# Attention in rounds of four chunks, with one scaling per output group and GpSimd copying the gate's columns

## The chip, the core and the metric

The kernel runs on one core of a Trainium2 chip. The metric is device time in microseconds for one launch. One execution was also recorded by the hardware profiler; all durations below come from that recording.

## The reference

The computation is a linear attention over 8 batches, 8 heads, 576 positions and head dimension 64, followed by a mixture of 8 experts with sticky routing:

```python
def phi(x):                                   # 64 -> 128 -> 256 features
    proj = x @ w_phi
    proj = proj - max(abs(proj), axis=-1)
    return concatenate([exp(proj), exp(-proj)])
kv  = einsum('bhsf,bhsd->bhfd', phi(k), v)
z   = sum(phi(k), axis=s)
out = (phi(q) @ kv) / (phi(q) @ z + 1e-6)     # (B, H, S, D) -> x (B, S, 512)
# per token: logits = x @ w_gate; a local gate decides between argmax(logits)
# and the expert of the token before; p = softmax; out = p[e] * (relu(x @ w1[e]) @ w2[e])
```

All inputs and outputs are float32.

## The kernel before

**Attention.** Two batches and two heads form a unit; there are 16 units (`NBP` x `NHP`), each of 9 chunks (`NC`) of 128 positions, 144 chunks in all. Chunk 4 of a unit is split between the two batches, called b = 0 and b = 1. Two consecutive chunks form a pair, 72 pairs. The order of TensorE's instructions is written out by hand; the other engines are ordered by a scheduler that respects the data and the buffers.

`step(p)` is called once per pair and issues on TensorE, in this order:

- `proj(p)`: the projections of keys and queries of a pair into the tile `pj` (2 PSUM buffers). VectorE takes the maximum of absolute values (`m`, L186) and subtracts it (`sb`, L188); ScalarE makes the key features `kp` (L192).
- `qtr(p-1)`: four transposes of the queries' part into `qt` (1 PSUM buffer), from which ScalarE makes the query features `qp` (two instructions, L206; 8 buffers).
- `turn` and then `gate` of what became ready in earlier steps: when the last chunk of a unit's batch half has been summed, `kv_end` copies the sum out (ScalarE, `kf` and `kvs`). `turn`, one step later, transposes it (L251) into a PSUM tile `nm` and ScalarE copies that out (`ks`, L254). `gate`, again one step later, multiplies it with the gate's weights (L263) into another `nm` tile, and ScalarE copies the nine columns into `kvs` (L265). This tile then also receives the first group of outputs.
- `kv` of the two chunks of pair p-2 (L225, tile `kvp`).
- up to `QUOTA` = 18 entries of the list `todo`. An entry is one matrix multiplication of `num` (two records in the profile, L284), eight entries per chunk. A `num` covers two or three chunks and one `nm` tile; there are four per unit, on chunks (0,1), (2,3), (4,5,6) and (7,8). Its last entry, `end`, issues the scaling: VectorE adds 1e-6 to the denominators (L301), inverts them (L302), scales the 64 output columns of both heads into `xo` (L306) and the nine gate columns into `lg` (L308); one DMA on SyncE's queue writes `xo` to the tensor `xs` (L312).
- what `kv` has left after a unit's half was completed, and then the background work: the routing of a finished pair of batches (`gate(bp)`, a generator started by `ends`, which is an entry of `todo` too), and early preparation of experts. It advances piece by piece, has small matrix multiplications into a tile that shares the one PSUM buffer of `qt` (`pst`), and loads and splits expert weights (L753, L754).

The `nm` tiles have **two** PSUM buffers, shared by `turn`, `gate` and `num`. GpSimd scatters the routing lists and gathers tokens with indirect DMAs; `paced` puts a small copy (`tick`, L387) in front of each of these, which waits for `m`.

**Experts.** After the attention come the expert slots: each loads 4 MB of weights, splits them in a high and a low part on ScalarE and VectorE (L753, L754), and TensorE multiplies in three products (L799 to L801).

Of the kernel before, what the change touches and what calls it, by code (L numbers as in the profile page):

```python
# [6 lines left out]
F32 = mybir.dt.float32  # L7
# [9 lines left out]
B, H, S, D = 8, 8, 576, 64  # L17
# [10 lines left out]
WAIT = 5  # L28
LAG = 2
WE, WR, WL = 8, 4, 1  # L30
FILL = 6
KVLAG = 2
QUOTA = 18

STEP = "step"

# [10 lines left out]
class Kernel:  # L47
# [9 lines left out]
    def run(self):  # L57
        nc, tc, A = self.nc, self.tc, self.A
        act, dve = self.act, self.dve
        with ExitStack() as root:  # L60
            self.const = self.mkpool(root, "const", 1, "left")
            dram = self.mkpool(root, "dram", 1, "left", DRAM)
            self.xs = dram.tile([NT + 1, DM], F32, name="xs")

            self.lst = dram.tile([E * NT + 128, 2], F32, name="lst")
            first = self.const.tile([128, 256], F32, name="first")
            self.sp.dma_start(first[:, 128:256], A["first"][:, 384:512])
            self.ident, self.w2 = first[:, 0:128], first[:, 128:256]
            self.cnt = self.const.tile([128, E], BF16, name="cnt")
            dve.memset(self.cnt, 0.0)  # L70

            warm = self.const.tile([128, E], BF16, name="warm")
            act.activation(warm, self.cnt, AF.Exp)

            self.wgi = self.const.tile([128, NHP, 2, 9], F32, name="wgi")
            self.pool.memset(self.wgi, 0.0)

            self.vs = [[self.const.tile([128, 2, D + 1], F32, name=f"vs{k}{b}") for b in (0, 1)] for k in (0, 1)]
            for x in self.vs:
                for t in x:  # L80
# [12 lines left out]
            self.psf = self.mkpool(front, "psf", 2, "right", PSUM)  # L93
            self.wphases = [(self.moe_early, WE)]

            self.scattering = False
            self.tail, self.eslots, self.scattered = False, [], []
            self.g, self.ch, self.kvb, self.lg = {}, {}, {}, {}
            n = NBP * NHP * NC
            self.todo, self.turns, self.gates, self.background = [], [], [], []  # L100
            self.fetched = 0
            for gi in range(3):
                self.fetch_kqv(gi)
                if gi == 0:
                    self.sp.dma_start(first[:, 0:128], A["first"][:, 256:384])
                    self.consts()
            with tc.manual_schedule(engines={mybir.EngineType.PE}):
                for p in range(n // 2):
                    while self.fetched < n // 3 and self.fetched * 3 < 2 * p + 8:
                        self.fetch_kqv(self.fetched)  # L110
                    if p == FILL:
# [3 lines left out]
                    self.step(p, n)  # L115
            self.tail = True
            p = n // 2
            while p < n // 2 + KVLAG + 1 or self.todo or self.turns or self.gates:
                self.step(p, n)
                p += 1  # L120
# [51 lines left out]
    def proj(self, p):  # L172

        dve, act = self.dve, self.act

        t = self.psf.tile([128, 2, 2, 2, 128], F32, name="pj")
        for i in (2 * p, 2 * p + 1):
            kq = self.g[i // 3]["kq"]
            s = slice(i % 3 * 128, i % 3 * 128 + 128)
            for j in (0, 1):  # L180
                for h in (0, 1):
                    r = slice(64 * h, 64 * h + 64)
                    self.last_pe = self.pe.matmul(t[:, h, i % 2, j, :], kq[r, j, s], self.w2[r], start=True, stop=True)  # L183
        m = self.m = self.front3.tile([128, 8], F32, name="m")
        f = t.rearrange("p h c j f -> p (h c j) f")
        dve.tensor_reduce(m, f, AX.X, ALU.max, apply_absolute_value=True)  # L186
        sb = self.front3.tile([128, 2, 2, 2, 128], F32, name="sb")
        self.last_dve = dve.tensor_sub(sb.rearrange("p h c j f -> p (h c j) f"), f,  # L188
                                       m.unsqueeze(2).broadcast_to([128, 8, 128]))
        kp = self.front3.tile([128, 2, 2, 2, 128], F32, name="kp", bufs=4)  # L190
        for sg in (0, 1):
            self.last_act = act.activation(kp[:, :, :, sg, :].rearrange("p c h f -> p h c f"), sb[:, :, :, 0], AF.Exp,  # L192
                                           scale=1.0 - 2 * sg)
        for c in (0, 1):
            self.ch[2 * p + c] = dict(kp=kp[:, c], sb=sb)
# [76 lines left out]
    def num(self, u, b, cs, kvs, bank=None):  # L272
# [22 lines left out]
        def end():  # L295
            last()
            dve, t = self.dve, e["t"]
            for c in cs:
                del self.ch[u * NC + c]
            rc = self.back2.tile([128, 3, 2], F32, name="rc", bufs=3)[:, 0:n]  # L300
            dve.tensor_scalar_add(rc, t[:, :, :, D], 1e-6)  # L301
            dve.reciprocal(rc, rc)  # L302
            if hp == 0 and c0 == 0:
                self.lg[bp] = self.back2.tile([128, NC, 9, H], F32, name="lg")
            xo = self.back2.tile([128, 3, 128], F32, name="xo", bufs=4)[:, 0:n]
            dve.tensor_mul(xo.rearrange("p c (h d) -> p c h d", h=2), t[:, :, :, 0:D],  # L306
                           rc.unsqueeze(3).broadcast_to([128, n, 2, D]))
            dve.tensor_mul(self.lg[bp][:, c0:c0 + n, :, 2 * hp:2 * hp + 2].rearrange("p c e h -> p c h e"),  # L308
                           t[:, :, :, D + 1:KV], rc.unsqueeze(3).broadcast_to([128, n, 2, 9]))
            r0 = bp * TB + c0 * 128  # L310
            dst = self.xs[r0:r0 + n * 128, hp * 128:hp * 128 + 128].rearrange("(c p) d -> p c d", p=128)
            self.sp.dma_start(dst, xo)  # L312
        self.todo.append(end)

    def ends(self, bp):
# [29 lines left out]
                self.load(s, i)  # L345
            yield

    def step(self, p, n):

        if p < n // 2:  # L350
            self.proj(p)
        if 0 <= p - 1 < n // 2:
            self.qtr(p - 1)
        gates, self.gates = self.gates, []
        turns, self.turns = self.turns, []
        for x in turns:
# [1 line left out]
        for x in gates:  # L358
            x()
        parts = [[]]  # L360
        if 0 <= p - KVLAG < n // 2:
            for i in (2 * (p - KVLAG), 2 * (p - KVLAG) + 1):
                a, *more = self.kv(i)
                parts[-1] += a
                parts += more
        for x in parts[0]:
            x()
        for _ in range(min(QUOTA, len(self.todo)) if p < n // 2 else len(self.todo)):
            self.todo.pop(0)()
        for part in parts[1:]:  # L370
            for x in part:
                x()
        for x in list(self.background):
            for _ in range(6):
                y = next(x, self)
                if y is self:
                    self.background.remove(x)
                if y is self or y is STEP:
                    break

    def paced(self):
# [5 lines left out]
        return self.tc.issue_after(self.pool.tensor_copy(t, self.m[:, 0:1]).ins)  # L387


    def pst(self, shape):  # L390
# [617 lines left out]
```

## Time and profile before

| | |
|---|---|
| median of 3 runs | 834.18 us (828.74 to 838.76) |
| profiled execution, its own time | 827.13 us |
| its span, first to last instruction | 825.4 us |
| TensorE matmuls busy | 788.1 us (95%) |
| VectorE busy | 555.4 us (67%) |
| ScalarE busy | 428.2 us (52%) |
| GpSimd busy | 146.7 us (18%) |
| attention | about the first 335 us of the span |

Busy time is the union of an engine's instructions; matmuls are pipelined, so a TensorE that is busy all the time may still be waiting for short spells. The weight loads of TensorE (PEld) are shown beside its matmuls (PE) and show its issue rhythm more sharply. "Released by" names the work whose end let an instruction start; "issue" is idle time for which the profile shows no cause.

### The profile page before, as it was taken

Reading aid. Unit: us, or ns where it says so; the run is one execution under the profiler, and the core shown is the slowest. Engines: PE = TensorE matmul, PEld = TensorE weight load, DVE = VectorE, ACT = ScalarE, POOL = GpSimd, SP = SyncE. Lnnn points to the kernel's source line nnn. Section 1 sums busy time; section 2 is a strip of 40 time slices with the busy share of each in tenths; the row PEclk is TensorE's granted clock in tenths of the full one; section 3 lists DMA queues with packets and bytes.
Section 4 is the critical chain, followed back from the end, with each engine's and each line's share of the span. In section 5 each row is a group of like instructions: output and inputs, shape, how many; then the busy total and the mean of one; then the engine's idle time right before and its main releaser. Section 6 shows DMA issues by size and latency. Waiting matters only on the chain.

```text
span 825.4 us, 23470 instructions
## 1 busy us (share of the span) xinstructions
PE 788.1 (95%) x9777; PEld 710.0 (86%) x9777; DVE 555.4 (67%) x956; ACT 428.2 (52%) x738; POOL 146.7 (18%) x156
## 2 busy tenths in 40 slices
PE   6999998999989899888999999999999999999997
PEld 5899987898878788777898998998898898999896
DVE  5677897679878885848754444644686777568541
ACT  4666665566666565323543333533564557447431
POOL 0000002200231132051421202212122212201010
PEclk9999999999999999999999999999999999999999
DMA  6545546764799531574974433744696687767510
GB/s 193 141 123 135 144 130 92 124 149 126 151 215 236 168 102 36 157 138 136 393 255 141 162 116 121 286 141 148 207 346 211 209 319 263 257 224 273 192 44 23
DMA packets 74239, 145.01 MB, mean 176 GB/s; under 512 B 9198, under 2 KB 48757, under 8 KB 74112
## 3 DMA queue, kind: packets, MB, share of 16 engines
q1 hardware_dynamic: 66272, 123.14, 50.9%
q0 software_dynamic: 7792, 20.02, 7.2%
q8 instruction: 79, 1.29, 0.7%
q10 hardware_dynamic: 64, 0.30, 0.1%
q14 instruction: 32, 0.26, 0.1%
HBM read 124.51 MB, written 20.26 MB: 175 GB/s over the span
## 4 chain that ended last, share of the span: by engine, by line
PE 69%; issue 12%; DMA 7%; DVE 6%; ACT 2%; POOL 2%; another core or an unknown queue 1%; SPq 1%; POOLq 0%; DVEq 0%; ACTq 0%
PE l L799 12%; PE l L800 12%; PE l L801 12%; PE kvp L225 8%; PE pj L183 8%; PE nm L284 8%; PE qt L203 4%; DMA out<-y,p_tokm 4%; DMA wraw<-in_w2h 2%; PE tr L791 1%; DVE sb L188 1%; DVE m L186 1%; PE nm L263 1%; POOL out L874 1%; DMA p_lrm<-lst,p_rim 1%
## 5 line engine op out<-in xcount | busy, mean ns | idle before, releaser
L753 ACT CAST whi<-wraw 128x1024 fp32r<-128x1024 f32 x160 | 167.5, 1048 | 205.7 <-PE l L801 111.6
L754 DVE TENSOR_TENSOR wlo<-wraw,whi 128x1024 fp32r<-128x1024 f32 x160 | 195.7, 1224 | 85.9 <-ACT whi L753 83.6
L799 PE MATMUL l<-xhi,whi 128*128 128x256 f32 x544 | 155.2, 286 | 2.1 <-DVE hl L822 1.4
L800 PE MATMUL l<-xlo,whi 128*128 128x256 f32 x544 | 152.8, 281 | 0.3 <-DVE xlo L794 0.3
L801 PE MATMUL l<-xhi,wlo 128*128 128x256 f32 x544 | 152.4, 280 | 0.0
L799 PE MATMUL l<-whi,hh 128*128 128x512 f32 x320 | 127.4, 398 | 0.7 <-DVE y L873 0.7
L800 PE MATMUL l<-wlo,hh 128*128 128x512 f32 x320 | 125.8, 393 | 0.0
L801 PE MATMUL l<-whi,hl 128*128 128x512 f32 x320 | 125.7, 393 | 0.0
L186 DVE TENSOR_REDUCE m<-pj 128x8 f32<-128x1024 f32 x72 | 87.9, 1220 | 43.9 <-PE pj L183 43.7
L206 ACT ACTIVATE qp<-qt 128x512 f32<-128x512 f32 x144 | 84.7, 604 | 60.3 <-PE qt L203 57.9
L192 ACT ACTIVATE kp<-sb 128x512 f32<-128x512 f32 x144 | 82.9, 623 | 54.2 <-DVE sb L188 46.5
L799 PEld LDWEIGHTS l<-xhi,whi 128*128 128x128 f32 x544 | 102.8, 189 | 4.5 <-DVE hl L822 1.9
L800 PEld LDWEIGHTS l<-xlo,whi 128*128 128x128 f32 x544 | 102.8, 189 | 1.1 <-DVE xlo L794 0.5
L801 PEld LDWEIGHTS l<-xhi,wlo 128*128 128x128 f32 x544 | 102.9, 189 | 0.0
L284 PE MATMUL nm<-kvs,qp 128*64 128x74 f32 x2304 | 89.0, 230 | 6.8 <-ACT kvs L265 4.8
L183 PE MATMUL pj<-first,kq 64*128 64x128 f32 x1152 | 86.9, 291 | 8.1 <-DMA kq<-in_kqT 6.4
L874 POOL DMA_INDIRECT out<-y,p_tokm x34 | 44.4, 1305 | 269.2 <-DVE y L873 250.7
L188 DVE TENSOR_TENSOR sb<-pj,m 128x1024 f32<-128x1024 f32 x72 | 88.1, 1224 | 3.7
L284 PEld LDWEIGHTS nm<-kvs,qp 128*64 128x64 f32 x2304 | 81.2, 139 | 8.1 <-ACT kvs L265 5.3
L183 PEld LDWEIGHTS pj<-first,kq 64*128 64x128 f32 x1152 | 72.6, 193 | 13.9 <-issue 6.8
L225 PE MATMUL kvp<-v,kp 128*64 128x65 f32 x2048 | 78.1, 227 | 0.5 <-ACT kvs L245 0.4
L225 PEld LDWEIGHTS kvp<-v,kp 128*64 128x64 f32 x2048 | 68.5, 140 | 6.6 <-issue 5.4
(200 smaller groups left out, 1000.3 us busy)
## 6 DMA issues: line engine op xcount, KB each, us to landing
wraw<-in_w1h SPq DMA_DIRECT2D x80, 512.0 KB, 5.9
wraw<-in_w2h SPq DMA_DIRECT2D x80, 512.0 KB, 4.4
kq<-in_kqT SPq DMA_DIRECT2D x47, 384.0 KB, 4.6
v<-in_va SPq DMA_DIRECT2D x48, 195.0 KB, 3.0
xs<-xo SPq DMA_DIRECT2D x48, 128.0 KB, 4.1
xs<-xo SPq DMA_DIRECT2D x16, 192.0 KB, 2.1
vs<-in_va SPq DMA_DIRECT2D x32, 32.5 KB, 3.0
lst<-pr,ri POOLq DMA_INDIRECT x36, 6.3
```

Source lines behind the costliest of these rows:

```text
L183: self.last_pe = self.pe.matmul(t[:, h, i % 2, j, :], kq[r, j, s], self.w2[r], start=True, stop=True)
L186: dve.tensor_reduce(m, f, AX.X, ALU.max, apply_absolute_value=True)
L188: self.last_dve = dve.tensor_sub(sb.rearrange("p h c j f -> p (h c j) f"), f, m.unsqueeze(2).broadcast_to([128, 8, 128]))
L192: self.last_act = act.activation(kp[:, :, :, sg, :].rearrange("p c h f -> p h c f"), sb[:, :, :, 0], AF.Exp, scale=1.0 - 2 * sg)
L206: self.act.activation(qp[:, sg], t, AF.Exp, scale=1.0 - 2 * sg)
L225: self.pe.matmul(self.kvp[r, sg, h], self.ch[i]["kp"][:, h, sg, r], self.v(i, b)[:, h], start=first and n < 2, stop=last and n >= 6)
L284: self.pe.matmul(e["t"][r, c - c0, h, :], self.ch[i]["qp"][:, sg, h, q0 + r.start:q0 + r.stop], kvs[:, sg, h, :], start=sg == 0, stop=sg == 1)
L753: self.act.copy(hi, raw)
L754: self.dve.tensor_sub(lo, raw, hi.bitcast(F32))
L799: mm(o, ah, bh, start=first, stop=False)
L800: mm(o, ah, bl, start=False, stop=False)
L801: self.last_pe = mm(o, al, bh, start=False, stop=last)
```

## The change

Attention is stepped in rounds of two pairs (four chunks), 36 of them. In a round i TensorE issues `proj(2i)` and `proj(2i+1)`, `qtr(2i-1)`, `turn`, `gate`, `kv` of the four chunks of the round before, up to 32 entries of `todo` (before: 18 per pair), the rest of `kv`, background work, `qtr(2i)`, and background work again. In `end`, one VectorE instruction scales all 74 columns of both heads into a wider `xo` (5 buffers instead of 4), GpSimd copies the nine gate columns into `lg`, one copy for each head, and two DMAs write the outputs, one for each head, with runs of 64 instead of 128 columns. `kp` has 5 buffers instead of 4.

```diff
-FILL = 6
-KVLAG = 2
-QUOTA = 18
+FILL = 3
+QUOTA = 32
...
-                for p in range(n // 2):
-                    while self.fetched < n // 3 and self.fetched * 3 < 2 * p + 8:
+                for i in range(n // 4):
+                    while self.fetched < n // 3 and self.fetched * 3 < 4 * i + 10:
...
-        m = self.m = self.front3.tile([128, 8], F32, name="m")
+        m = self.m[p % 2] = self.front3.tile([128, 8], F32, name="m")
...
-        kp = self.front3.tile([128, 2, 2, 2, 128], F32, name="kp", bufs=4)
+        kp = self.front3.tile([128, 2, 2, 2, 128], F32, name="kp", bufs=5)
...
-            xo = self.back2.tile([128, 3, 128], F32, name="xo", bufs=4)[:, 0:n]
-            dve.tensor_mul(xo.rearrange("p c (h d) -> p c h d", h=2), t[:, :, :, 0:D],
-                           rc.unsqueeze(3).broadcast_to([128, n, 2, D]))
-            dve.tensor_mul(self.lg[bp][:, c0:c0 + n, :, 2 * hp:2 * hp + 2].rearrange("p c e h -> p c h e"),
-                           t[:, :, :, D + 1:KV], rc.unsqueeze(3).broadcast_to([128, n, 2, 9]))
+            xo = self.back2.tile([128, 3, 2, KV], F32, name="xo", bufs=5)[:, 0:n]
+            dve.tensor_mul(xo, t, rc.unsqueeze(3).broadcast_to([128, n, 2, KV]))
+            for h in (0, 1):
+                self.pool.tensor_copy(self.lg[bp][:, c0:c0 + n, :, 2 * hp + h], xo[:, :, h, D + 1:KV])
             r0 = bp * TB + c0 * 128
-            dst = self.xs[r0:r0 + n * 128, hp * 128:hp * 128 + 128].rearrange("(c p) d -> p c d", p=128)
-            self.sp.dma_start(dst, xo)
+            for h in (0, 1):
+                at = hp * 128 + h * 64
+                dst = self.xs[r0:r0 + n * 128, at:at + 64].rearrange("(c p) d -> p c d", p=128)
+                self.sp.dma_start(dst, xo[:, :, h, 0:D])
...
-    def step(self, p, n):
-        if p < n // 2:
-            self.proj(p)
-        if 0 <= p - 1 < n // 2:
-            self.qtr(p - 1)
+    def step(self, i, n):
+        last = n // 2
+        for p in (2 * i, 2 * i + 1):
+            if p < last:
+                self.proj(p)
+        if 0 <= 2 * i - 1 < last:
+            self.qtr(2 * i - 1)
         gates, self.gates = self.gates, []
         turns, self.turns = self.turns, []
         for x in turns:
...
         parts = [[]]
-        if 0 <= p - KVLAG < n // 2:
-            for i in (2 * (p - KVLAG), 2 * (p - KVLAG) + 1):
-                a, *more = self.kv(i)
+        for c in range(4 * i - 4, 4 * i):
+            if 0 <= c < n:
+                a, *more = self.kv(c)
                 parts[-1] += a
                 parts += more
         for x in parts[0]:
             x()
-        for _ in range(min(QUOTA, len(self.todo)) if p < n // 2 else len(self.todo)):
+        for _ in range(min(QUOTA, len(self.todo)) if i < n // 4 else len(self.todo)):
             self.todo.pop(0)()
         for part in parts[1:]:
             for x in part:
                 x()
+        self.chores(0)
+        if 2 * i < last:
+            self.qtr(2 * i)
+        self.chores(1)
+
+    def chores(self, k):
+        self.half = k
         for x in list(self.background):
...
-        return self.tc.issue_after(self.pool.tensor_copy(t, self.m[:, 0:1]).ins)
+        return self.tc.issue_after(self.pool.tensor_copy(t, self.m[self.half][:, 0:1]).ins)
```

More of the change, by code (lines that the diff above doesn't have):

```diff
@@ L96, in run @@
             self.scattering = False
-            self.tail, self.eslots, self.scattered = False, [], []
+            self.tail, self.eslots, self.scattered, self.m = False, [], [], [None, None]
             self.g, self.ch, self.kvb, self.lg = {}, {}, {}, {}
@@ L107, in run @@
             with tc.manual_schedule(engines={mybir.EngineType.PE}):
[L108 to L109 removed]
+                for i in range(n // 4):
+                    while self.fetched < n // 3 and self.fetched * 3 < 4 * i + 10:
                         self.fetch_kqv(self.fetched)
[L111 removed]
+                    if i == FILL:
                         with tc.issue_after(self.last_act.ins):
@@ L114, in run @@
                             act.dma_start(self.lst, A["fill"])
-                    self.step(p, n)
+                    self.step(i, n)
             self.tail = True
[L117 to L120, printed above, removed]
+            i = n // 4
+            while i < n // 4 + 2 or self.todo or self.turns or self.gates:
+                self.step(i, n)
+                i += 1
             for x in self.background:
```

## The prediction, made before the changed kernel was run

> **What bounds the kernel now.** I read the engines' shares first, then busy time by stretch (from and to, length, then busy us and count of PE, PEld, VectorE, ScalarE and GpSimd, the granted clock, DMA share, GB/s): the attention without its ends, the experts, and the part of the attention in which expert weights come in.
>
> ```profile
> span 825.4 us, 23470 instructions
> PE 788.1 (95%) x9777; PEld 710.0 (86%) x9777; DVE 555.4 (67%) x956; ACT 428.2 (52%) x738; POOL 146.7 (18%) x156
> ...
> 20.00:322.00 302.00, 287.04 (x6242) 258.23 (x6241) 242.39 (x517) 189.12 (x407) 39.26 (x60) 0.99 0.60 141
> ...
> 345.00:826.00 481.00, 468.64 (x3046) 423.20 (x3044) 286.77 (x375) 221.51 (x300) 105.62 (x86) 1.00 0.59 200
> ...
> 220.00:300.00 80.00, 72.23 (x1532) 64.77 (x1528) 66.79 (x141) 50.78 (x105) 19.38 (x27) 0.98 0.81 202
> ```
>
> The change touches the attention alone (the first 335 us); the 481 us of experts stay. From 20 to 322 us TensorE's matmuls are busy 287 of 302 us, VectorE 242. TensorE is the bound, with 15 us of idle time, 8 of them from 220 to 300 us (72 of 80 busy), where VectorE has 67 of 80. What TensorE waits for in the attention that VectorE causes is little (us in total, times, the longest); the next rows are shorter:
>
> ```profile
> PE nm L251 <- DVE lg L308: 1.7, 1, 1.7
> PE qt L203 <- DVE rc L301: 0.9, 2, 0.5
> ```
>
> So a shorter VectorE instruction brings next to nothing by itself; what counts is how densely TensorE issues. A steady pair, by its weight loads (start, duration), and what ScalarE and VectorE do beside it:
>
> ```profile
> 161.30 0.97 PEld L183 LDWEIGHTS pj<-first,kq 64*128 64x128 f32 x16
> 162.39 0.42 PEld L203 LDWEIGHTS qt<-first,sb 128*128 128x128 f32 x4
> 162.98 0.31 PEld L263 LDWEIGHTS nm<-wgi,ks 128*64 128x64 f32 x8 [0.17 <-issue]
> 163.21 1.02 PEld L225 LDWEIGHTS kvp<-v,kp 128*64 128x64 f32 x32
> 164.14 1.23 PEld L284 LDWEIGHTS nm<-kvs,qp 128*64 128x64 f32 x36
> 165.45 0.30 PEld L183 LDWEIGHTS pj<-first,kq 64*128 64x128 f32 x4
> ...
> 163.65 0.62 ACT L206 ACTIVATE qp<-qt 128x512 f32<-128x512 f32 x1
> ...
> 162.58 1.23 DVE L186 TENSOR_REDUCE m<-pj 128x8 f32<-128x1024 f32 x1 [0.53 <-PE pj L183]
> 163.84 1.22 DVE L188 TENSOR_TENSOR sb<-pj,m 128x1024 f32<-128x1024 f32 x1
> ```
>
> A pair takes 165.45 - 161.30 = 4.15 us. Only three changes of kind leave a gap: after `pj` 0.12 (162.39 less 161.30 + 0.97), after `qt` 0.17, after `nm` 0.08: 0.37 us.
>
> **Rounds: fewer changes of kind.** Two pairs have 0.74 us of gaps now. A round has `pj`-`qt` 0.12, `qt`-next 0.17, `nm`-`qt` (taken as `nm`-`pj`, 0.08) and `qt`-`pj` (as `qt`-next, 0.17): 0.54. It saves 0.20 us; times 36, **-7 us**. The bounds are 0 (if the new neighbours cost what the old ones did) and 36 x 0.37 = -13 (a whole pair's gaps). VectorE's lateness shrinks too: `qt` now comes about four us after its `sb`, so the small `qt` and L251 waits above may go: **-3** (0 to -3).
>
> **Rounds: what queues at the two `nm` buffers.** This part decides. I counted the order from the code. A unit half is summed in round c/4 + 1 (rounded down; c its last chunk), turned one round later and gated one later still. Halves end 4 and 5 chunks apart, so now `turn` of one half and `gate` of the half before stand back to back in nearly every round; with pairs they never met in one step. And 32 entries a round are exactly the four chunks that arrive, so the backlog never drains (with 18 a pair against 16 arriving it did): entries left after rounds 4 to 12 are 0, 8, 8, 16, 16, 24, 24, 33, 1. In round 13 the entry `ends` takes one place, and from then on every round stops one or more entries short of some `num`'s end. That `num` keeps its buffer over the round's boundary, `turn` takes the other, and `gate` must wait until ScalarE has copied `turn`'s tile. This holds in rounds 6, 7, 10, 14 to 19, 22 to 28 and 31 to 36: 22 rounds. TensorE issues in order, so `kv`, `num`, `qt` and the next `pj` stand behind. In the tail a gate waits for a turn's copy already:
>
> ```profile
> 330.49 0.20 PEld L251 LDWEIGHTS nm<-first,kf 128*128 128x128 f32 x2 [0.68 <-issue]
> 331.39 0.31 PEld L263 LDWEIGHTS nm<-wgi,ks 128*64 128x64 f32 x8 [0.70 <-ACT ks L254]
> ```
>
> An undisturbed turn and what follows it, and ScalarE's copy of that turn:
>
> ```profile
> 150.25 0.38 PE L251 MATMUL nm<-first,kf 128*128 128x128 f32 x2
> 150.57 1.15 PE L225 MATMUL kvp<-v,kp 128*64 128x65 f32 x32
> ```
>
> ```profile
> 150.95 0.37 ACT L254 COPY ks<-nm 128x256 f32<-128x256 f32 x1
> ```
>
> From the turn to what follows it, 0.90 us with the wait and 0.32 without: 0.58 us, with ScalarE free (with `qp` ahead of the copy it ends at 151.32, 1.07 after the turn, so 0.75). 22 x 0.58 = **+13 us** (up to 17; the lower end 0 would need the buffers to come free otherwise).
>
> In rounds 10, 17, 18, 19, 26, 27, 28, 35 and 36 one buffer is the gate's, whose `num` is not yet next, so a `num` needs the very buffer that the `num` just finished leaves, through VectorE:
>
> ```profile
> 151.55 1.07 PE L284 MATMUL nm<-kvs,qp 128*64 128x74 f32 x28
> ```
>
> ```profile
> 152.67 0.16 DVE L301 TENSOR_SCALAR rc<-nm 128x4 f32<-128x4 f32 x1 [0.24 <-PE nm L284]
> ...
> 153.08 0.42 DVE L306 TENSOR_TENSOR xo<-nm,rc 128x256 f32<-128x256 f32 x1
> 153.42 0.21 DVE L308 TENSOR_TENSOR lg<-nm,rc 128x36 f32<-128x36 f32 x1
> ...
> 161.33 0.56 DVE L306 TENSOR_TENSOR xo<-nm,rc 128x384 f32<-128x384 f32 x1
> ```
>
> ```profile
> 273.32 0.41 PE L251 MATMUL nm<-first,kf 128*128 128x128 f32 x2 [1.65 <-DVE lg L308]
> ```
>
> 128 more columns cost 0.56 - 0.42 us, 1.1 ns each, so the wide scaling takes 0.42 + 40 x 1.1 ns = 0.46 us. The matmuls end at 152.62, `xo` would end at 153.54, and a restart adds about 0.1: 1.0 us each, 9 us in all. The last row shows such a wait in the kernel before, 1.65 us with VectorE busy. In rounds 11, 20 and 29 only one chunk's `kv` stands ahead of `todo`, so the `num` ends about 5 us into the round (two `pj` 2.0, `qt` 0.6, turn and wait 0.9, gate 0.2, `kv` 0.5, half a `num` 0.6) while VectorE is on the four 1.23 us instructions of both pairs until 1.0 + 4.9 = 5.9: up to 2 us each; I take 1.7, 5 us. Together **+14** (0 to 20).
>
> **Rounds: the routing's small matmuls.** About 15 of them (four for each of three routings, three for the early experts) use `qt`'s single buffer. Before, they stood a `kv` and `num` behind `qt` and a `pj` ahead of the next. Now about half follow `qtr(2i)` directly and wait for both `qp` instructions: `qt` at 162.39, the second ends at 164.27, 1.88 us, less the 0.59 to the next load, 1.29 us; the others stand just ahead of `qtr(2i)`, which waits for VectorE's copy, as here:
>
> ```profile
> 276.43 0.28 PE L432 MATMUL pt<-first,g_code 128*9 128x128 f32 x1 [0.39 <-DVE p_probe L580]
> ```
>
> 8 x 1.29 + 7 x 0.39 = **+13** (3, the seven short waits alone, to 20).
>
> **The clock.** Idle spells have slowed TensorE before:
>
> ```profile
> 246.16 0.93 PE L183 MATMUL pj<-first,kq 64*128 64x128 f32 x10 [1.69 <-issue]
> 247.70:251.00 3.30, 3.30 (x56) 3.09 (x56) 3.06 (x4) 1.64 (x4) 2.02 (x2) 0.50 0.88 237
> ```
>
> After a wait of 1.69 us the granted clock was 0.50 for 3.3 us, which costs 1.7. I count one more: **+2** (0 to 9, five such spells). The Trainium skill ("TensorE: Matmul & The Clock Gate", Part 1) has the clock halved after an idle window of about 3.4 us; by it, waits of 1 or 2 us would cost nothing more, and this term would be 0. The rows above speak against taking the rule that strictly.
>
> **The outputs.** On VectorE 0.42 + 0.21 = 0.63 us become 0.46: 0.17 x 64 = 11 us of its 242 are saved, covered by TensorE's work, so 0 beyond the -3 above; if VectorE were the bound it would be all 11. GpSimd gets 128 small copies, SyncE 64 more issues:
>
> ```profile
> L387 POOL COPY tick<-m 128x1 f32<-128x1 f32 x28 | 6.9, 245 | 250.1 <-DVE m L186 229.3 <-DVE g_fr L420 11.4 <-DVE p_ohf L625 3.9
> ```
>
> ```profile
> q1 hardware_dynamic: 66272, 123.14, 50.9%
> ```
>
> 128 x 0.245 = 31 us on a GpSimd that is busy 39 of 302. A copy may queue behind a scatter; five `xo` buffers, nearly three rounds, hide that, and only the routing's first sum of `lg` waits for it, once on the tail's path: **+0.5** (0 to 3). The 64 extra issues hold SyncE, and its loads are fetched ahead by rounds: 0. The queue took 50.9% of the span for 123 MB, 3.4 us per MB, so the 9.4 MB of outputs (4608 x 512 floats) take 32 us of a DMA share of 0.60: covered even if they doubled; only at 220 to 300 us (0.81, 0.92 then) might it cost, 0 to 4. The Trainium skill ("DMA: Bandwidth & Descriptors", Specifications) names 512 B as the least transfer at line rate, with a read-modify-write below. The new runs have 256 B; if that doubles the stores' time, this is the case just bounded. No run here shows it.
>
> ```profile
> 152.47 1.15 ACT L192 ACTIVATE kp<-sb 128x512 f32<-128x512 f32 x2 [0.65 <-DVE sb L188]
> ```
>
> ScalarE's `qp` is short of buffers: from round 14 a ninth pair is alive when `qtr(2i-1)` asks for one, so its `qp` starts only with the round's first `num` entries, and then stands against `kp` (1.15 us for two) ahead of `qtr(2i)`. At worst 22 x 0.9 us; about 2 us of `num` lie between, which cover most: **+2** (0 to 20).
>
> **Sum.** -7 - 3 + 13 + 14 + 13 + 2 + 0.5 + 2 = +34.5 us, on the profiled execution's 827.1 (span 825.4, 1.7 around it): 862. The median of the three runs is 7 higher; one of the three is near the profile. I leave 862 as the forecast; from the median it would be 869. Bounds of the likely case: about half of the waits, 845, and nearly all upper ends together, 890.
>
> **Rivals.** (1) *Faster: the waits aren't there.* If the backlog stayed clear of the buffers, through stalls elsewhere or a release order other than the one I count, 827 - 7 - 3 = 817, and with half of the idle time at 220 to 300 us gone 813. For it: VectorE loses 11 us and TensorE's 15 us idle might shrink. Against: two buffers, and the order is fixed. It decides if the three queueing terms sum to under 10 us. (2) *No change:* ScalarE and VectorE release sooner and a third of the 40 us remains, 827 - 10 + 13 = 830. (3) *VectorE takes TensorE's place:* the 4.9 us of two pairs in one block, with weights split in between (1.2 us each), hold the release of `nm` and then of `pj`; each of the 36 rounds then loses another half us, 880 to 890. (4) *GpSimd's queue:* copies behind scatters hold `xo` and so VectorE; at most 10 us on top. That the rounds aren't formed is excluded, as TensorE's order is by hand.
>
> Chances: forecast 0.52, (3) and (4) 0.12, (2) 0.14, (1) 0.22. Something over 1% (8 us) is what a measurement of this kernel can tell. Faster 0.22, same 0.14, slower 0.64. The range runs from 812, which takes in the faster case, to 886.
>
> **What would show it.** Right: `gate` (L263) waiting for `ks` L254 in some 20 rounds; L284 waiting for the scaling in about 12; small `pt` matmuls waiting for `qp`; the attention 25 to 45 us longer, the experts as long as before. Wrong: TensorE's waits in the attention under 15 us and rounds near 8 us. Most in doubt is how soon ScalarE and VectorE release a buffer.

## The result, and the profile after

The changed kernel takes **886.12 us** (median of 4 runs, 883.64 to 889.53) against 832.55 us for the kernel before in the same comparison (828.74 to 838.76): a ratio of **1.0675, 95% interval 1.0636 to 1.0715**. It is slower, by 53.6 us where 34.5 were forecast; the spans of the two profiled executions differ by 885.8 - 825.4 = 60.4 us. The forecast of 862 us starts from the profiled execution of the kernel before (827.1 us), which was 5.4 us below the median here.

The page of the changed kernel, its span and the engines' shares:

```profile
span 885.8 us, 23584 instructions
...
PE 791.8 (89%) x9777; PEld 716.1 (81%) x9777; DVE 554.2 (63%) x892; ACT 427.2 (48%) x738; POOL 166.5 (19%) x281
```

TensorE's work is what it was (9777 matmuls, 792 us busy against 788), but its share fell from 95 to 89%: it waits. Where, the busy time by stretch tells (columns as in the prediction), attention and experts of the changed kernel:

```profile
20.00:380.00 360.00, 297.61 (x6456) 270.69 (x6454) 248.67 (x474) 194.13 (x418) 58.28 (x180) 0.97 0.49 123
395.00:885.00 490.00, 468.55 (x3017) 422.26 (x3016) 283.83 (x365) 219.37 (x297) 106.43 (x88) 0.98 0.58 195
```

In the attention TensorE is now idle for 62 of 360 us, against 15 of 302 before, while VectorE is busy for 249 of 360, 69%: no engine took TensorE's place. The second row hides more idle time: in the experts it is 21.5 of 490 us against 12.4 of 481. What TensorE waited for, in the changed kernel (us in total, times, the longest):

```profile
PE nm L283 <- DVE xo L306: 21.8, 13, 3.9
PE pt L587 <- DMA p_lrf<-lst,p_rif: 12.3, 1, 12.3
PE nm L262 <- ACT ks L253: 12.1, 22, 1.6
PE kvp L224 <- ACT kvs L244: 6.5, 7, 1.7
PE pj L182 <- DMA kq<-in_kqT: 6.5, 2, 4.7
PE nm L283 <- DVE rc L300: 4.4, 5, 1.3
PE pt L452 <- ACT qp L205: 3.5, 3, 1.2
PE pt L476 <- ACT qp L205: 3.5, 3, 1.2
```

The 22 rounds in which a `gate` waits for its neighbour's `ks` are there, and by the starts of `pj` they are the very rounds that the prediction counted; `num` waits for the scaling in 18 places, 21.8 + 4.4 = 26.2 us. The second row wasn't foreseen at all: one wait of 12.3 us in the experts, for the early list's fetch.

I also added up every gap between the starts of successive matmuls, from 20 us to the first matmul of the experts: what a gap has over 0.26 us (0.36 where the kind changes) counts as waiting, less the 0.06 (0.20) that it has anyway; the remainder is time to issue. "Half clock" is time in which the granted clock was 0.50.

| us | 20 to first expert matmul | waits | issue | first expert matmul to the end | at half clock in the attention |
|---|---|---|---|---|---|
| before | 317.9 | 20.7 | 297.2 | 487.5 | 6.8 |
| after | 365.4 | 72.6 | 292.8 | 500.4 | 23.9 |

So 60.4 = 51.9 more of waits - 4.4 of issue + 12.9 in the experts. The issue time holds 17.1 us more at half clock, which cost up to 8.6; without them the rounds would save up to 13 us.

### The profile page after: what moved, and what is told of

It reads as the page before. It is cut to its first block, busy times and chain, and to the rows that moved or that the text cites. A ratio compares the mean times of both kernels' runs of the same rounds, so it can differ in the third digit from the quotient of the medians.

```text
span 885.8 us, 23584 instructions
## 1 busy us (share of the span) xinstructions
PE 791.8 (89%) x9777; PEld 716.1 (81%) x9777; DVE 554.2 (63%) x892; ACT 427.2 (48%) x738; POOL 166.5 (19%) x281
## 3 DMA queue, kind: packets, MB, share of 16 engines
q1 hardware_dynamic: 85728, 123.14, 46.5%
## 4 chain that ended last, share of the span: by engine, by line
PE 46%; DVE 13%; issue 13%; DMA 9%; ACT 3%; POOL 3%; SPq 0%; POOLq 0%; DVEq 0%; ACTq 0%
PE l L809 11%; PE l L810 11%; PE l L811 10%; PE nm L283 4%; DVE m L185 4%; DVE sb L187 4%; DMA out<-y,p_tokm 4%; PE kvp L224 3%; PE pj L182 3%; DMA wraw<-in_w1h 2%; PE qt L202 2%; PE tr L801 1%; ACT qp L205 1%; DMA kq<-in_kqT 1%; DVE xo L306 1%
## 5 line engine op out<-in xcount | busy, mean ns | idle before, releaser
L283 PE MATMUL nm<-kvs,qp 128*64 128x74 f32 x2304 | 92.2, 237 | 28.5 <-DVE xo L306 21.8
L205 ACT ACTIVATE qp<-qt 128x512 f32<-128x512 f32 x144 | 80.5, 595 | 65.9 <-PE qt L202 65.1
L283 PEld LDWEIGHTS nm<-kvs,qp 128*64 128x64 f32 x2304 | 85.8, 145 | 31.5 <-issue 26.6
L191 ACT ACTIVATE kp<-sb 128x512 f32<-128x512 f32 x144 | 86.8, 630 | 39.8 <-DVE sb L187 38.5
L182 PE MATMUL pj<-first,kq 64*128 64x128 f32 x1152 | 80.1, 291 | 7.0 <-DMA kq<-in_kqT 6.5
L224 PE MATMUL kvp<-v,kp 128*64 128x65 f32 x2048 | 73.7, 225 | 5.1 <-ACT kvs L244 2.6
```

Source lines behind the costliest of these rows:

```text
L205: self.act.activation(qp[:, sg], t, AF.Exp, scale=1.0 - 2 * sg)
L224: self.pe.matmul(self.kvp[r, sg, h], self.ch[i]["kp"][:, h, sg, r], self.v(i, b)[:, h], start=first and n < 2, stop=last and n >= 6)
L283: self.pe.matmul(e["t"][r, c - c0, h, :], self.ch[i]["qp"][:, sg, h, q0 + r.start:q0 + r.stop], kvs[:, sg, h, :], start=sg == 0, stop=sg == 1)
```

## The experiments

Medians are given with the ratio to the kernel before of the same comparison; two kernels are compared with each other by these ratios.

**The outputs alone, and the rounds alone.** One run has the rounds with the old outputs (two scalings on VectorE, one store); the other the single pairs with the new outputs. The first against the kernel after, its core:

```diff
-            xo = self.back2.tile([128, 3, 2, KV], F32, name="xo", bufs=5)[:, 0:n]
-            dve.tensor_mul(xo, t, rc.unsqueeze(3).broadcast_to([128, n, 2, KV]))
-            for h in (0, 1):
-                self.pool.tensor_copy(self.lg[bp][:, c0:c0 + n, :, 2 * hp + h], xo[:, :, h, D + 1:KV])
+            xo = self.back2.tile([128, 3, 128], F32, name="xo", bufs=4)[:, 0:n]
+            dve.tensor_mul(xo.rearrange("p c (h d) -> p c h d", h=2), t[:, :, :, 0:D],
+                           rc.unsqueeze(3).broadcast_to([128, n, 2, D]))
+            dve.tensor_mul(self.lg[bp][:, c0:c0 + n, :, 2 * hp:2 * hp + 2].rearrange("p c e h -> p c h e"),
+                           t[:, :, :, D + 1:KV], rc.unsqueeze(3).broadcast_to([128, n, 2, 9]))
...
-            for h in (0, 1):
-                at = hp * 128 + h * 64
-                dst = self.xs[r0:r0 + n * 128, at:at + 64].rearrange("(c p) d -> p c d", p=128)
-                self.sp.dma_start(dst, xo[:, :, h, 0:D])
+            dst = self.xs[r0:r0 + n * 128, hp * 128:hp * 128 + 128].rearrange("(c p) d -> p c d", p=128)
+            self.sp.dma_start(dst, xo)
```

The second is the same diff the other way round, in the kernel before.

> Rounds alone, outputs scaled and stored as before. Theory 'buffers' (the loss comes from the queue at the two nm buffers that the rounds make): 884 to 892 us, the gate columns' own scaling (0.2 us) now being inside the release of a buffer. Rival 'outputs' (the wide scaling, GpSimd's copies or the 256-byte runs cost the time): 30 us or more below the changed kernel.

> Outputs alone, on the kernel before with its steps of one pair. 'Buffers': within 4 us of the kernel before (832.6), as VectorE's saved 11 us are covered. 'Outputs': 850 us or more.

Measured: rounds with old outputs 886.45 us, 1.0703 (1.0647 to 1.0760), the same as the kernel after. Pairs with new outputs 822.46 us, **0.9924 (0.9891 to 0.9957)**: the output part for itself makes the kernel a little faster, by 6.7 us where at most 4 were expected, and the whole loss is the rounds'. As the gain is under 1%, it was timed again in five rounds:

> The kernel before with the new outputs alone (one wide scaling, gate columns copied by GpSimd), the same as the second run of this study, timed again in five rounds because its gain there (ratio 0.9924) is under 1%. If the gain is real: ratio 0.988 to 0.997. If it was the luck of that call: an interval that takes in 1.0.

Measured: 823.55 us, 0.9956 (0.9920 to 0.9992). This version beats both kernels. By the matmuls' starts its attention is 4 us shorter (first expert matmul at 334.1 and 333.9 us against 337.9). The stretch of the attention in the first of these runs:

```profile
20.00:318.00 298.00, 284.81 (x6229) 255.81 (x6226) 237.80 (x459) 187.70 (x406) 60.69 (x176) 0.99 0.62 142
```

TensorE's idle time is 13 us instead of 15. VectorE was spared the 11 us of the prediction: up to the first expert matmul its instructions add up to 275.2 us, before to 286.2. In the profiled executions the experts give most of it back (490.9 us against 487.5, with 12.5 us at half clock against 0.8), so that the spans, 825.0 and 825.4, hardly differ; the gain rests on the timed runs.

**The list emptied.** One number of the kernel after changed, so that no `num` is left over a round's boundary:

```diff
-QUOTA = 32
+QUOTA = 40
```

> The changed kernel with up to 40 entries of todo per round instead of 32, so that every round empties the list and no num holds a buffer over the boundary. 'Buffers': the 22 waits of gate for ks (12 us), the 18 of num for the scaling (26 us) go, and the routing starts a round earlier, which may bring back the early list's late fetch (13 us): 832 to 850 us. Rival 'the rounds' own shape' (five us of VectorE work in one block, waits that only change place): 875 us or more, with the waits of L283 still there.

Measured: 847.63 us, 1.0229 (1.0179 to 1.0279). Its waits of `kvp` and `pt`, and what is left of `gate` for `ks` (22 waits, 12.1 us in the kernel after); `num` for the scaling is no longer among the waits:

```profile
PE kvp L224 <- ACT kvs L244: 10.6, 5, 3.6
...
PE pt L452 <- ACT qp L205: 3.5, 3, 1.2
PE pt L476 <- ACT qp L205: 3.5, 3, 1.2
...
PE nm L262 <- ACT ks L253: 0.5, 1, 0.5
```

Waits in the attention fell from 72.6 to about 44 us, and the 12.3 us in the experts are gone (491.0 to the end instead of 500.4). The leftover is thus needed for the `num` and `gate` waits and for the late fetch. What remains, +15.1 us in the attention against the kernel before, is mostly `kvp` for its copy (15 us more between successive `kvp` matmuls than before): where the list is empty, only a few matmuls stand between the end of one unit's half and the next half's first `kv`. In the longest of these waits, up to 273.86 us, ScalarE's copies of `kvp` queue behind a `kp` that waited for VectorE's subtraction.

A second run with 40 entries had the routing's steps ahead of `qt` too:

```diff
         self.chores(0)
+        self.chores(1)
         if 2 * i < last:
             self.qtr(2 * i)
-        self.chores(1)
```

> Rounds with 40 entries, and both parts of the background work ahead of qtr(2i) instead of one on each side. Theory 'the shared qt buffer': six waits of the small matmuls for qp, 1.2 us each, become waits of some 0.4 us for VectorE: 4 to 7 us less than with 40 entries alone (847.6). Rival (they wait as long for VectorE): within 2 us.

Measured: 844.25 us, 1.0136 (1.0083 to 1.0190). Waits about 41 us: the 7 us of `pt` for `qp` became 5.5 of `pt` for VectorE. Rounds without a leftover stay slower than single pairs.

**Is it the leftover alone?** The kernel before, with 16 entries a pair, exactly what arrives, so that its list can't drain either:

```diff
-QUOTA = 18
+QUOTA = 16
```

> The kernel before (single pairs, old outputs) with 16 list entries a pair instead of 18, so that the list can't drain: exactly what arrives is taken, as with 32 a round in the kernel after. Theory (the leftover of the list at the step's end is the main cause, rounds of two pairs only make VectorE's block longer): num and gate waits of 15 to 40 us appear with single pairs too, the last routing comes late, and the time is 845 to 870 us. Rival (it is the pairing of pairs that does it: turn and gate in one step and a block of two pairs): the waits in the attention stay under 25 us altogether, time 828 to 838 us.

Measured: 836.36 us, 1.0081 (1.0038 to 1.0125). My theory fell, and the rival holds: in the attention waits are 18.5 us against 20.7, and the first expert matmul at 335.5 us against 337.9. By the order of the code `turn` and `gate` don't meet in one step there, and two buffers suffice for what is left over. The whole loss is behind the attention, 498.4 us against 487.5, and its main row is:

```profile
PE pt L577 <- DMA p_lrf<-lst,p_rif: 10.5, 1, 10.5
```

This run isolates the late fetch. The fetch needs the last routing's list; the routing starts when `ends` comes up in the list, and with a leftover that is late. The issue of the fetch in the kernels before and after:

```profile
L565 POOL DMA_INDIRECT p_lrf<-lst,p_rif x1: 888/888/888, 325.4 to 325.4; - x1
```

```profile
L575 POOL DMA_INDIRECT p_lrf<-lst,p_rif x1: 887/887/887, 415.2 to 415.2; - x1
```

At 325.4 the fetch lies 26 us ahead of the matmul that needs it (351.6); at 415.2 the matmul (417.5) waits for it. With 16 entries a pair it goes out at 365.9 us, with 40 a round at 330.2.

**The routing hurried in the tail.** The kernel after, with the background advanced more often once the chunks are through:

```diff
         self.chores(1)
+        if self.tail:
+            self.chores(0)
+            self.chores(1)
```

> The changed kernel with the background work advanced twice as often in the three rounds of the tail, so that the early list's fetch is issued ahead of the last routing's nine scatters. Theory 'late list' (the fetch p_lrf waits for these scatters, which put 12.3 us of TensorE's waiting into the experts): 870 to 877 us, with p_lrf issued before the last routing's scatters. Rival (the wait is only taken over by the gather or the list's next reader): 882 us or more.

Measured: 887.82 us, 1.0688 (1.0621 to 1.0756): no gain. The fetch went out at 372.0 us, its wait is gone and the rest is 492.1 us, 8.3 shorter; but the attention is 6.9 us longer:

```profile
PE nm L262 <- ACT ks L253: 18.3, 22, 7.8
```

One of the 22 waits, at the end of the last round, is now 7.8 us long: ScalarE was idle for 8.96 us ahead of the copy, until an event that the profile doesn't name. So the fetch's wait can be taken away, but what then lengthened the attention stays open.

**Where a `num` wait comes from.** A round of the kernel after, with one of its long waits (start, duration, engine, line, idle time before and its releaser; lines of the same stretch that don't bear on it are left out):

```profile
189.97 0.81 PE L283 MATMUL nm<-kvs,qp 128*64 128x74 f32 x18
...
190.40 1.21 DVE L185 TENSOR_REDUCE m<-pj 128x8 f32<-128x1024 f32 x1
...
191.53 0.15 DVE L300 TENSOR_SCALAR rc<-nm 128x4 f32<-128x4 f32 x1
...
191.72 1.23 DVE L187 TENSOR_TENSOR sb<-pj,m 128x1024 f32<-128x1024 f32 x1
...
192.86 0.17 DVE L301 RECIPROCAL rc<-rc 128x4 f32<-128x4 f32 x1
...
193.06 0.47 DVE L306 TENSOR_TENSOR xo<-nm,rc 128x296 f32<-128x296 f32 x1
...
193.68 1.63 PE L283 MATMUL nm<-kvs,qp 128*64 128x74 f32 x22 [2.89 <-DVE xo L306]
```

The `num` ends at 190.78, and its buffer comes free at 193.53, 2.75 us later, because VectorE has the second pair's maximum and subtraction in between. Undisturbed, the prediction had 0.92 for this (matmuls end 152.62, scaling ends 153.54). But most of the 18 waits are not like this one. Laid against VectorE's rows, VectorE's other long instructions (maximum, subtraction, a split of weights) lie between the end of the `num` and the end of the scaling for 10.6 us over all 18, of which 7.4 are in three waits (at 101, 194 and 287 us); the rest is the three short instructions themselves and TensorE's restart. Nor did the release become slower: over all 64 `num`, from the last matmul to the end of the last scaling, it takes 1.40 us on average before and 1.39 after. What is new is that TensorE needs that very buffer.

Five runs change one thing each around this place. `turn` ahead of the round's projections:

```diff
     def step(self, i, n):
+        gates, self.gates = self.gates, []
+        turns, self.turns = self.turns, []
+        for x in turns:
+            x()
...
-        gates, self.gates = self.gates, []
-        turns, self.turns = self.turns, []
-        for x in turns:
-            x()
```

> The changed kernel with turn issued ahead of the round's two pj instead of right ahead of gate, so that ScalarE's copy of the turn lies beside pj. 'Buffers': the waits of L262 for ks (12 us) go, those of num stay: 870 to 878 us. Rival (the wait only moves on to num or turn): 883 us or more.

Measured: 889.18 us, 1.0728 (1.0672 to 1.0784), not the gain expected; the rival, which had 883 us or more, holds:

```profile
PE nm L283 <- DVE xo L306: 28.9, 13, 3.8
...
PE nm L283 <- DVE rc L300: 6.6, 6, 1.3
...
PE nm L283 <- DVE rc L301: 5.5, 3, 2.5
...
PE nm L262 <- ACT ks L253: 0.5, 1, 0.5
```

The gate's 12 us are gone, and the `num` waits grew by 13.9 (41.0 with the third row, which had 0.9 before): TensorE only reaches the busy buffer earlier.

Next, the gate not at the round's head but in the list, eight entries ahead of its end, and not counted in a round's 32 (the core of the edit):

```diff
         for x in gates:
-            x()
+            self.todo.insert(max(len(self.todo) - 8, 0), x)
```

> The kernel after, with the gate's matmuls not at the round's head but in the list, eight entries ahead of its end at that time; turn stays at the head, and the gates don't count in the 32 entries of a round. The leftover of the list stays as it was, and so does VectorE's block of both pairs. Theory (a gate at the head takes one of the two nm buffers long before its num is next, so that the leftover's nums go one after the other through the single buffer that is left): the num waits for the scaling fall from 26.2 to under 12 us, the gate's waits for ks from 12.1 to under 5, the attention ends 15 to 30 us earlier (first expert matmul at 355 to 370 us instead of 385.4), the rest stays near 500 us, time 855 to 872 us. Rival (VectorE's block sets the release, wherever the gate stands): the waits move on to another place and the time is 880 to 895 us. In rounds with a short list, kvs may be waited for behind the gate, up to 36 x 0.3 us.

Measured: 890.78 us, 1.0656 (1.0581 to 1.0732): the rival's time. Waits 69.3 us; by the matmuls' starts, `num` behind `num` fell from 30.4 to 15.5 us, but `gate` behind `num` took 19.1 and `num` behind its own gate 6.5. A place in that run:

```profile
195.51 0.70 PEld L283 LDWEIGHTS nm<-kvs,qp 128*64 128x64 f32 x18 [0.16 <-issue]
...
196.72 0.16 DVE L300 TENSOR_SCALAR rc<-nm 128x4 f32<-128x4 f32 x1
...
196.80 1.22 DVE L187 TENSOR_TENSOR sb<-pj,m 128x1024 f32<-128x1024 f32 x1
...
198.13 0.47 DVE L306 TENSOR_TENSOR xo<-nm,rc 128x296 f32<-128x296 f32 x1
...
198.75 0.41 PE L262 MATMUL nm<-wgi,ks 128*64 128x18 f32 x8 [2.38 <-DVE sb L187]
```

It is the same release, with the subtraction ahead of the scaling; only the instruction that meets it is another.

Then, half of the maximum's columns left out, so that VectorE's block is shorter (the result then routes other tokens and the experts take longer; the attention alone is judged), and the same in the kernel before as a control:

```diff
-        dve.tensor_reduce(m, f, AX.X, ALU.max, apply_absolute_value=True)
+        dve.tensor_reduce(m, f[:, :, 0:64], AX.X, ALU.max, apply_absolute_value=True)
```

> The changed kernel with the maximum m taken over half of the columns (leaves out the other half), which makes each L185 about 0.6 us shorter and the VectorE block of a round 1.2 us. Theory 'VectorE sets the release' (a num waits for its buffer because the scaling queues behind the block of both pairs): the 27 us of L283's waits fall to under 17 and the whole to 862 to 876 us. Rival 'turnaround' (each wait is the time from the last matmul through the three short instructions, with VectorE free): 881 us or more.

> The control: the same half of the maximum left out of the kernel before. VectorE loses 41 us there, which TensorE's work covers: 3 to 8 us less than the kernel before, from 220 to 300 us alone. If VectorE were a bound of the steps of one pair: 15 us less or more.

Measured: 939.61 us, its attention not shorter but 10.4 us longer (first expert matmul at 395.8 us against 385.4); the control 871.33 us, its attention 2.4 us longer where 3 to 8 less were expected, so VectorE's time is covered there. In the first:

```profile
PE nm L262 <- ACT ks L253: 26.5, 21, 2.4
PE nm L283 <- DVE xo L306: 16.9, 12, 2.1
```

With a third row (`rc` L301: 0.9 us in the kernel after, 1.1 here) the `num` waits fell from 27.1 to 18.0 us, and those of `gate` for ScalarE rose from 12.1 to 26.5: with the shorter maximum a `kp` of 0.63 us starts ahead of ScalarE's copy of the turn in most rounds (at 159.41 us, the copy at 159.94), where in the kernel after the copy mostly starts 0.04 us after the turn. One further wait of a `gate`, 5.6 us, has no cause that the profile shows.

Next, the second pair's projection itself in the middle of the list's entries:

```diff
-        for p in (2 * i, 2 * i + 1):
-            if p < last:
-                self.proj(p)
+        if 2 * i < last:
+            self.proj(2 * i)
...
+            if k == QUOTA // 2 and second:
+                second.pop()()
             self.todo.pop(0)()
```

> The kernel after, with the round's second pair of projections issued behind the first 16 entries of the list instead of at the round's head. VectorE then has one pair's maximum and subtraction (2.4 us) in one place and the other's in another, instead of 4.9 us together. Theory (VectorE's block of both pairs holds back the scaling that releases an nm buffer): the num waits for the scaling (21.8 + 4.4 us in the kernel after) fall below 12 us and the attention becomes 10 to 25 us shorter (first expert matmul at 360 to 375 us instead of 385.4), although a change of kind comes back in each round (36 x 0.1 to 0.2 us = 4 to 7 us); the backlog stays, so the early list's fetch stays late (rest of the run 495 to 501 us); time 860 to 875 us. Rival (the waits come from the two nm buffers and the list's leftover alone, whoever is busy): num waits stay above 22 us, time 882 to 895 us.

Measured: 906.23 us, 1.0957 (1.0874 to 1.1040): neither theory's time. The `num` waits for the scaling fell to 17.9 us, but only one projection now lies between the two `qt` of neighbouring rounds, `qt` waits 19.4 us for `qp` (1.5 before), and 53 more changes of kind came in. The run is inconclusive, since it added a wait of its own.

Three of these runs moved TensorE's instructions, and one shortened VectorE's. The last pair leaves TensorE's order as it is and moves VectorE's alone: the second pair's maximum and subtraction are held behind the round's first scaling (block of one pair, scaling, block of the other, scaling). The run after it does so with 40 entries and the routing ahead of `qt`. The core of the edit:

```diff
-            self.todo.pop(0)()
+            x = self.todo.pop(0)
+            x()
+            if second and x.__name__ == "end":
+                with self.tc.issue_after(self.scaled.ins):
+                    second()
+                second = None
```

> The kernel after, with TensorE's order unchanged and VectorE's order alone changed: the maximum and subtraction of the round's second pair come behind the first scaling of the round (block of one pair, scaling, block of the other pair, scaling). Theory (VectorE's block of both pairs ahead of the scaling sets the release of the nm buffers): the waits of num for the scaling fall from 26.2 to under 12 us, the attention ends 10 to 25 us earlier (first expert matmul at 360 to 375 us instead of 385.4), the gate's waits for ks stay near 12 us, the rest near 500 us; time 862 to 878 us. Rival (the two buffers' order alone): num waits stay over 20 us, time 880 to 895 us. A second rival: the later block makes the second pair's tiles late, and the waits come back at qt or pj: num waits under 12 us, but qt or pj waits over 10 us, time 878 to 900 us.

> The same with 40 list entries a round and the routing's steps ahead of qt, as in the eighth run of this study (844.25 us). There num waits for the scaling hardly stand any more, so by the theory VectorE's order should bring little: 838 to 846 us; the waits of kvp for its copy (about 10 to 17 us in the runs with 40) stay. Rival (VectorE's block holds the rounds back in other ways too, through the release of pj and through kp): under 836 us, near the kernel before.

Measured: 884.77 us, 1.0674 (1.0609 to 1.0739), no faster than the kernel after. Its waits (here L287 is `num`, L310 the scaling, L266 `gate`, L206 `qt`):

```profile
PE nm L287 <- DVE xo L310: 14.2, 12, 2.1
...
PE nm L266 <- ACT ks L257: 11.0, 22, 0.7
...
PE qt L206 <- ACT qp L209: 5.7, 12, 1.3
...
PE nm L287 <- DVE rc L305: 1.1, 1, 1.1
```

The `num` waits fell from 27.1 to 15.3 us and the longest from 3.9 to 2.1. That is near the 10.6 us that VectorE's rows gave for its block; the two ways agree. None of the three forecasts for this run fits whole: the waits lie between theirs, and the time is that of the two rivals, for `qt`, `pt` and `pj` wait longer for tiles that come later (`qt` for `qp` 4.2 us more; `pt` and `qt` around each other 3 more; `pj` for `sb` 2.1), and the attention gains 3.1 us (382.3 against 385.4). With 40 entries the hold is a clear loss: 866.36 us, 1.0455 (1.0389 to 1.0521), against 1.0136 without it; the routing's `pt` waits for VectorE rose from 5.8 to 13.5 us, those within `pj` from 1.4 to 10.4, and 54.6 us ran at half clock. Both forecasts for that run failed.

## Why the prediction was right and wrong

The direction was right, and so was the mechanism of the waits at the `nm` buffers, down to the rounds. 862 us was too low by 24: 5.4 of them are the profiled execution from which the sum starts, and 19 the change. Two steps failed: the term of `num` waiting for the scaling was sized 12 us too small, and the experts, which were to stay, took 12.9 us more. The range ends at 886 and the measured time is 886.12; its runs go from 883.64 to 889.53, so on which side of that end it fell was luck. Step by step:

- **Fewer changes of kind, -7 (0 to -13):** issue time fell by 4.4 us with up to 8.6 us of half clock in it, so the step itself lies between -4 and -13, inside its range. The runs don't separate it further. **VectorE's lateness, -3:** the waits from `pj` to `qt` and from `qt` to `turn` shrank by 1.2 and 2.1 us; right.
- **Gate behind turn, 22 x 0.58 = 13:** 22 waits, 12.1 us (mostly 0.46 each, the longest 1.6); 13.7 by the matmuls' starts. Right.
- **`num` waiting for the scaling, 14 (0 to 20):** 26.2 us, beyond the upper end. This is the term that was mis-sized. Rounds 11, 20 and 29, taken at 1.7 us each for VectorE's block, waited 3.0, 2.9 and 3.9 us: 9.8 instead of 5. Of the nine rounds at 1.0 us, eight have such a wait (the last one none), 11.5 us instead of 9. Seven rounds that the count left out (14, 15, 22 to 24, 31 and 32) took 4.9 us; why they wait too was not worked out. So pricing the release undisturbed was near, and the block, longer than estimated in three rounds, and the missing rounds made the rest. Rival (3) gave 880 to 890 us, which the kernel hit, for such a block in each of the 36 rounds, but it isn't as that rival had it: the block is worth 10.6 us in `nm`, VectorE isn't the bound (69% busy), and `pj` hardly waited.
- **Routing's matmuls, 13:** about 10 us; 6 of them waited for `qp`, not 8. Near. **`qp` short of buffers, +2:** 1.5 us. Right.
- **The clock, +2 (0 to 9):** up to 8.6 us in the attention, the upper end, as more waits stood to set it off.
- **Outputs, +0.5:** right inside the rounds (1.0703 with the old ones, 1.0675 with the new); for themselves they gain 0.4 to 0.8%. The wide scaling took 0.466 us, as worked out. GpSimd's copies held up the routing's first sum of `lg` (L419) by 0.8 us in all. The stores were not free, but nothing shows that anything waited for them. The queue's row in the kernel after:

```profile
q1 hardware_dynamic: 85728, 123.14, 46.5%
```

46.5% of 885.8 is 412 us, against 50.9% of 825.4, 420 us, before: 19456 more packets, and the queue took no longer in total. That hides a cost of the stores, since the packets of the loads took less time in the longer run. Added up from the trace's packet records, the 18432 packets of 512 B took 27 ns each before and the 36864 of 256 B 18 ns each after: 32 us of the 16 engines' time became 42, a third more, inside the doubling that the prediction bounded. The runs with the rounds alone and the outputs alone have the same 27 and 18 ns. The Trainium skill ("DMA: Bandwidth & Descriptors", Specifications) names a read-modify-write under 512 B. Whether that is it, or a fixed time per packet, no run here separates.

- **"The 481 us of experts stay":** wrong, +12.9 us. This step failed outright: the term stood at nothing, without a reason beyond the change's touching the attention alone. The prediction counted `ends` in the list that never drains, but didn't follow that to the last routing, its list and the fetch that a matmul early in the experts needs. The run with single pairs and 16 entries shows the term by itself: 10.9 us more, of which one wait is 10.5.
- **Not in the sum:** `kvp` waiting for its copy, 5 us.

The terms together: `num` 27.8, gate 13.7, routing 10.0, `kvp` 5.0, other waits 2.4 - 7.0, issue -4.4, experts 12.9: 60.4 us by the spans. What stays open is how much of the attention's remaining loss without a leftover (15 us) goes back to the pairing itself; no run removed the `kvp` waits.

## What to carry to other kernels

A list that feeds an in-order engine must drain a little faster than it fills: what it carries over a step's boundary costs nothing while a buffer is spare, holds scarce buffers as soon as two consumers meet in one step, and delays everything that stands at the list's end, here a fetch in the next phase. When a buffer's release goes through another engine, count the places where it is needed at once, and add that engine's block where it falls into one: of 26.2 us here, 16 were the undisturbed release and 10.6 the block. And don't add up waits as if each could be removed: five of the runs took 9 to 15 us off one wait; one of them gained 3 us in the attention and the others lost 2 to 18, since much of what TensorE met next was late as well, through VectorE or ScalarE. Batching two steps saved the issue gaps that it promised, and lost at least four times as much in waits.

## What the hardware showed that I had not expected

The half-clock spells are on a grid. In the kernel after the attention's spells start at 100.85, 193.01, 285.17, 326.12 and 363.67 us, all whole multiples of 3.41 us apart (27, 27, 12 and 11 of them). Two stretches, the spell at 193 and the one behind it:

```profile
193.00:196.40 3.40, 2.73 (x44) 2.76 (x45) 0.87 (x5) 1.22 (x3) 0.74 (x3) 0.50 0.23 52
196.40:199.80 3.40, 3.40 (x87) 3.17 (x85) 0.43 (x1) 0.59 (x2) 0.35 (x2) 1.00 0.40 91
```

In the 3.41 us ahead of that spell matmuls ran for 1.19 us, in the round shown above. I laid the grid over three traces (before, after, and the gate in the list): between 20 us and the last matmul every interval with under 1.5 us of matmuls was followed by half clock, none with over 2.3 was, and between these it went either way. The bounds are those of these traces: in the run with 40 entries and VectorE's order held, an interval that itself ran at half clock had 3.17 us of matmuls and was followed by another. By the bounds, a wait of 2 us in an otherwise busy stretch suffices where it falls into one interval, and does nothing where it straddles two evenly. The Trainium skill ("TensorE: Matmul & The Clock Gate", Part 1) has a free-running window of about 3.4 us, which the grid bears out; it has the clock halved after an idle window, where these rows show halving after windows with matmuls for more than a third of the time. This is why the prediction's clock term, counted by waits, was at the mercy of where they fell.
